# A fused attention, rational layer and expert layer on one core: weight conversion with PSUM banks and tiles of its own, weight words off GpSimd, two first steps moved, planner constants changed

## The chip, the core and the metric

The kernel runs on one core of a Trainium2 chip. The time is device microseconds of one execution; the kernel before is shown with the median of three runs and with one profiled execution, whose trace all rows below come from. In the rows, PE is TensorE's matmuls and PEld its weight loads, DVE is VectorE, ACT is ScalarE, POOL is GpSimd and SP is SyncE, which issues most DMAs.

## What is computed

Three layers follow each other. The first is a recurrence over 768 positions for 32 heads with a complex decay of bounded magnitude; the kernel computes it as chunked attention. The second is a rational function between two products (384 to 2048 to 384). The third routes each of the 3072 rows to one of eight experts and computes that expert's two products (384 to 1024 to 384).

```python
def _moe_ref(x, w_in, w_out, a, b):
    h = x @ w_in
    h2 = h * h
    h3 = h2 * h
    P = a[0] + a[1] * h + a[2] * h2 + a[3] * h3
    Q = 1.0 + np.abs(b[0]) * np.abs(h) + np.abs(b[1]) * h2
    g = P / (Q + 1e-06)
    return (g @ w_out).astype(np.float32)

def _moe2_ref(x, expert_emb, tau, w1, w2):
    xn = x / (np.linalg.norm(x, axis=-1, keepdims=True) + 1e-06)
    en = expert_emb / (np.linalg.norm(expert_emb, axis=-1, keepdims=True) + 1e-06)
    logits = xn @ en.T / tau
    expert_idx = np.argmax(logits, axis=1)
    ...
    for e in range(E):
        mask = expert_idx == e
        h = np.maximum(x[mask] @ w1[e], 0.0)
        out[mask] = gate_w[mask, None] * (h @ w2[e])
```

The weights of the rational layer come as 64 bit floats and are turned into 32 bit floats on the chip.

## The kernel before

The program is one straight line of instructions for each engine. Their order is written by a planner, `Plan`: a stage adds operations with an engine (or a choice of engines), an estimated duration, what they read and write, a due time, and sometimes a PSUM bank to take and to give back. `emit` then walks an estimated clock, takes among the operations that could start soonest the one with the earliest due time, and where there is a choice takes the engine with the lowest price (`price` times duration) or, if the operation is late, the one that ends first by estimate plus `bias`. An operation can only go where the planner put it: each engine works through its own list in order. There are two plans that matter here, one for `attention` and one for `mixture` (the rational layer and the expert slots); all of attention's instructions stand ahead of the mixture's in each engine's list.

**Attention** goes through 24 chunks of 128 rows. Its SBUF tiles come from three pools `a_p0` to `a_p2`, its eight PSUM banks from one pool `a_ps` that all of its steps share. Beside the chunks, `weight` (L680 on) converts the 32 weight tiles: a DMA into one of two `raw` tiles, an absolute value on ScalarE into one of two `wa` tiles, four VectorE steps through one bank, and for `w_out` a transpose and a small product, each with a bank of its own. The result lies in the `wf` tiles.

**The rational layer** runs over eight blocks of 384 columns with eight units each, 64 units in all. A unit (`unit`, L1020 on) is a first product `mm1` (18 matmuls, L1018) into one of the two `ph` banks pairs, six ScalarE and five VectorE steps (L1041 to L1053), and a second product `mm2` (18 matmuls, L1063) that is summed over the eight units in the `acc` banks. Unit 2 alone uses two `acc` banks for its first product. Numbers are split into a high and a low word: `split` (L1002) makes the high word `wh` by a cast (helper line L210) and the low word by a subtraction (L212) for each weight tile. Ten of the 32 tiles are split at the end of attention, 22 (11 high, 11 low) in this stage. `xsplit` does the same for a block of x (L229, L233). The planner's mark `free` stands for the release of attention's tiles and comes 9 us into the stage by its clock; it is an entry of the plan, not an instruction.

When a stage ends, its pools are released, and tiles of the next stage are laid over them; the first use of the new tile waits for the last users of what lay there. `mixture` takes its pools in the order `m_t`, `m_x`, `m_w`, `m_wh`, `m_g`, `m_r`, and its eight banks from one pool `m_ps`.

**The expert slots** follow: groups of 256 rows of one expert are gathered by GpSimd (L1358), transposed through `acc` banks (L1376), split (L982, L1381), multiplied with split weights (`slot_split`, L1414 for the low words) and scattered to the output (L1418). A small block for the last few rows of experts (L1548 to L1581) runs beside them.

```python
    def split(n):
        i, nm, lo = PARTS[n]
        on = [("A", 0.73), ("V", 0.47)] if not lo else [("V", 0.87), ("G", 1.76)]
```

## Time and profile before

| what | us |
|---|---|
| median of three runs | 945.04 |
| lowest and highest of them | 943.94, 947.12 |
| the profiled execution | 946.07 |
| its span, first to last instruction | 944.2 |

The rows below are read by stage. A busy time is the part of a stretch in which at least one instruction of the engine runs; the number in brackets is how many started there. PEclk is the granted clock of TensorE as a share of its higher level, 2.4 GHz; 0.50 is the lower level, 1.2 GHz, for the whole stretch. In a timeline, the brackets at the end of a row tell how long the engine stood idle before the instruction and whose work ended that.

### The profile page before, as it was taken

The numbers are of one execution on the slowest core, as the hardware profiler recorded it, in microseconds if no ns is written. First come the engines' busy times: TensorE is split into PE (matmuls) and PEld (weight loads), VectorE is DVE, ScalarE is ACT, GpSimd is POOL, SyncE is SP. The second block draws the span as 40 slices with busy tenths as digits, with TensorE's granted clock in tenths as the row PEclk, the third lists the DMA queues.
The fourth block names the chain that finished last, engine by engine and source line by source line (L and its number), as shares of the span: only waits on it lengthen the run. The fifth ranks groups of instructions, "written<-read, shape, count | busy, mean of one in ns | idle before, by whom it ended". The sixth has DMA issues, their size and how long they took to land. (4 is left out here: it accounts for less than half of the span.)

```text
span 944.2 us, 16850 instructions
## 1 busy us (share of the span) xinstructions
PE 877.2 (93%) x6119; PEld 834.0 (88%) x6119; DVE 738.1 (78%) x1419; ACT 704.3 (75%) x1134; POOL 237.1 (25%) x184
## 2 busy tenths in 40 slices
PE   2999999989879999999999999999998979999994
PEld 2788988878779999999999999999998878788994
DVE  7989998989799879787978888796987866556530
ACT  7989998989586988888988888888653543545530
POOL 2425434555254110001001010101322232225311
PEclk9999999989889999999999999999999998999997
DMA  9989988884200000010100000033202156551400
GB/s 174 200 174 175 184 187 175 151 188 100 85 1 1 1 26 1 1 26 1 26 1 26 1 27 1 16 77 94 35 9 60 51 163 204 171 168 37 168 26 27
DMA packets 172865, 76.41 MB, mean 81 GB/s; under 512 B 140840, under 2 KB 167352, under 8 KB 172772
## 3 DMA queue, kind: packets, MB, share of 16 engines
q1 hardware_dynamic: 168804, 65.58, 31.4%
q0 software_dynamic: 3968, 9.66, 3.6%
q8 instruction: 50, 0.82, 0.4%
q14 instruction: 43, 0.35, 0.2%
HBM read 92.19 MB, written 9.96 MB: 108 GB/s over the span
## 5 line engine op out<-in xcount | busy, mean ns | idle before, releaser
L1018 PE MATMUL ph<-xh,wi 128*128 128x384 f32 (+1 forms) x1284 | 306.2, 317 | 8.3 <-DVE wfi L490 4.2
L1018 PEld LDWEIGHTS ph<-xh,wi 128*128 128x128 f32 x1284 | 223.7, 190 | 10.3 <-DVE wfi L490 4.4
L1063 PE MATMUL acc<-wo,gh 128*128 128x392 f32 x768 | 202.0, 344 | 4.1 <-ACT gh L1052 4.1
L1018 PE MATMUL ph<-xl,wi 128*128 128x384 f32 (+1 forms) x642 | 203.1, 316 | 0.0
L1063 PEld LDWEIGHTS acc<-wo,gh 128*128 128x128 f32 x768 | 141.2, 190 | 4.4 <-ACT gh L1052 4.4
L1063 PE MATMUL acc<-wo,gl 128*128 128x392 f32 x384 | 131.7, 343 | 2.5 <-DVE gl L1053 2.5
L1018 PEld LDWEIGHTS ph<-xl,wi 128*128 128x128 f32 x642 | 122.0, 190 | 0.0
L1126 POOL DMA_INDIRECT idl<-tok,pos x24 | 24.6, 1026 | 281.4 <-DVE pos L1123 177.4
L1063 PEld LDWEIGHTS acc<-wo,gl 128*128 128x128 f32 x384 | 72.7, 189 | 3.3 <-DVE gl L1053 3.3
L1461 PE MATMUL acc<-wo,gh 128*128 128x384 f32 x256 | 70.0, 354 | 3.4 <-DVE wo L1414 3.4
L1053 DVE TENSOR_TENSOR gl<-u,gh 128x768 fp32r<-128x768 f32 x48 | 47.0, 979 | 27.1 <-PE acc L1063 26.2
L1041 ACT ACTIVATE sq<-ph,quad 128x768 f32<-128x768 f32 x43 | 38.8, 902 | 30.3 <-PE ph L1018 27.3
L1449 ACT ACTIVATE gh<-ph 128x512 fp32r<-128x512 f32 x36 | 21.6, 599 | 52.6 <-PE ph L1018 31.3
L1461 PEld LDWEIGHTS acc<-wo,gh 128*128 128x128 f32 x256 | 45.8, 194 | 9.1 <-issue 4.6
L499 ACT COPY qkT<-bank 96x512 f32<-96x512 f32 x96 | 50.7, 587 | 3.4 <-PE bank L621 3.0
L1418 POOL DMA_INDIRECT out_dram<-ah,ido x24 | 27.3, 1137 | 99.5 <-ACT ah L1466 55.2
L1358 POOL DMA_INDIRECT xT<-x2d,ids x24 | 27.2, 1134 | 98.9 <-DVE oh L1104 45.9
L630 PE MATMUL bank<-qkT 96*128 96x128 f32 x384 | 50.7, 279 | 1.3 <-ACT qkT L499 1.3
L1046 DVE SCALAR_TENSOR_TENSOR u<-u,qtmp,ph 128x768 f32<-128x768 f32 x47 | 47.2, 1005 | 5.4 <-ACT u L1044 5.3
L620 PE MATMUL bank<-cst,qf 128*96 128x128 f32 x192 | 48.2, 290 | 2.9 <-ACT qkT L499 2.9
L630 PEld LDWEIGHTS bank<-qkT 96*128 96x128 f32 x384 | 46.9, 193 | 2.8 <-ACT qkT L499 2.5
L1049 DVE SCALAR_TENSOR_TENSOR sq<-sq,quad,ah 128x768 f32<-128x768 f32 x43 | 46.6, 1084 | 0.6 <-ACT ah L1048 0.5
(298 smaller groups left out, 2160.6 us busy)
## 6 DMA issues: line engine op xcount, KB each, us to landing
xT<-in_moe_w_dram SPq DMA_DIRECT2D x24, 1536.0 KB
mw<-in_moe_w_dram SPq DMA_DIRECT2D x32, 384.0 KB
raw<-in_moe_w_out_dram SPq DMA_DIRECT2D x16, 384.0 KB
raw<-in_moe_w_in_dram SPq DMA_DIRECT2D x16, 384.0 KB
x2d<-rows SPq DMA_DIRECT2D x24, 192.5 KB
a_re<-in_a_re_dram SPq DMA_DIRECT2D x24, 192.0 KB
a_im<-in_a_im_dram SPq DMA_DIRECT2D x24, 192.0 KB
k<-in_k_dram SPq DMA_DIRECT2D x24, 192.0 KB
```

What stands on the lines that cost most here:

```text
L499: (A.copy if e == "A" else eng[e].tensor_copy)(o, i)
L620: T.transpose(pv[:, i, 0, :], Q[:, 2 * j + i, :], ident)
L630: T.matmul(pb(b)[:, i * P:(i + 1) * P], O[:, i, 1, :], O[:, i, 0, :], start=True, stop=True)
L1018: T.matmul(o, l, r, start=(n == 0), stop=(n == len(steps) - 1))
L1041: add(("A", 0.81 if many else 0.45), lambda e, c=c, h=h: A.activation(z[:, c], h(), AF.Abs, scale=coef.kb), w=kh + kz_)
L1046: add(("V", 0.93 if many else 0.53), lambda e, c=c, h=h: V.scalar_tensor_tensor(out=w[:, c], in0=w[:, c], scalar=coef.d, in1=h(), op0=ALU. ...
L1049: add(("V", 0.93), lambda e: V.scalar_tensor_tensor(out=z, in0=z, scalar=coef.e, in1=s, op0=ALU.add, op1=ALU.mult), r=ks, w=kz_)
L1053: add(("V", 0.87), lambda e: V.tensor_tensor(out=l, in0=w, in1=g.bitcast(F32), op=ALU.subtract), r=kw + kg, w=kl, lat=0.27)
L1063: T.matmul(o, x[:, j, sl], y("o", i)[:, c], start=(i == 0 and j == 0 and k == 0), stop=(i == NP - 1 and j == 1 and k == 2))
L1358: G.indirect_dma_start(out=xg[i][t], out_offset=None, in_=x2d[0:n, :], in_offset=bass.IndirectOffsetOnAxis(ap=ids[i][:, t:t + 1], axis=0), ...
L1418: G.indirect_dma_start(out=out[:, :], out_offset=bass.IndirectOffsetOnAxis(ap=dst, axis=0), in_=src, in_offset=None, bounds_check=NT - 1, ...
L1461: T.matmul(o, x[:, j, sl], w[:, c], start=(q == 0 and j == 0 and n == 0), stop=(q == NQ - 1 and j == 1 and n == 2))
```

## The change

- In attention, the PSUM pool is divided: six banks (`B`) for the chunks, two (`W`, a pool `a_psw`) for all banks that weight conversion takes. The tiles `raw` and `wa` come from a pool `a_w` that is allocated first.
- In `mixture`, `m_x` (the second x block) is allocated first and `m_t` second, so that `m_x` lies where `a_w` was. Two of the four `acc` banks come from a pool `m_psc` and lie where `a_psw` was; the two `ph` pairs and the other `acc` banks from `m_ps`.
- `split` has no choice of engine any more: high words on ScalarE, low words on VectorE.
- The memset of `seen` and the cast of `tok` were written ahead of the plan; they are now operations of it behind `free`. The split of x block 1 waits for `free` too.
- The planner's prices, biases and due times have new values.

```diff
-PRICE = {'A': 0.9451088, 'G': 0.6799360, 'V': 1.1, 'T': 0.0, 'S': 0.0}
+PRICE = {'A': 0.9451088, 'G': 0.5023880, 'V': 1.1, 'T': 0.0, 'S': 0.0}
-BIAS = {'A': -0.0773127, 'G': 0.1603192, 'V': 0.6045377, 'T': 0.0, 'S': 0.0}
+BIAS = {'A': -0.0215282, 'G': 0.2572650, 'V': 0.6045377, 'T': 0.0, 'S': 0.0}
-COST = {'A': 0.7094815, 'G': 0.3193946, 'V': 1.1, 'T': 0.0, 'S': 0.0}
-LEAN = {'A': 0.1119026, 'G': 0.1802717, 'V': 0.4995443, 'T': 0.0, 'S': 0.0}
-SPREAD = 0.0605191
+COST = {'A': 0.4040183, 'G': 0.5656184, 'V': 1.1, 'T': 0.0, 'S': 0.0}
+LEAN = {'A': -0.0850600, 'G': -0.1987378, 'V': 0.0905153, 'T': 0.0, 'S': 0.0}
+SPREAD = 0.1250329
-LEAN_FROM = 4.5359957
+LEAN_FROM = 3.1556660
...
-    STEP, SLACK, HALVED = 5.3246472, 0.0630705, (1,)
-    pools = [ctx.enter_context(tc.tile_pool(name=f"a_p{i}", bufs=1)) for i in range(3)]
-    ps = ctx.enter_context(tc.tile_pool(name="a_ps", bufs=1, space=PSUM))
+    NWB = 2
+    STEP, SLACK, HALVED = 5.3419923, 0.0630705, (1,)
+    late, *pools = (ctx.enter_context(tc.tile_pool(name=f"a_{n}", bufs=1)) for n in ("w", "p0", "p1", "p2"))
+    ps, psw = (ctx.enter_context(tc.tile_pool(name=n, bufs=1, space=PSUM)) for n in ("a_ps", "a_psw"))
...
-    raw = new("raw", [P, 384, 2], U32, c=2)
+    raw = [late.tile([P, 384, 2], U32, name=f"raw{i}") for i in range(2)]
-    wa = new("wa", [P, DM], c=2)
+    wa = [late.tile([P, DM], F32, name=f"wa{i}") for i in range(2)]
-    banks = [ps.tile([P, 512], F32, name=f"bank{i}") for i in range(8)]
...
+    banks = [(ps if i < 8 - NWB else psw).tile([P, 512], F32, name=f"bank{i}") for i in range(8)]
+    plan = Plan({"B": range(8 - NWB), "W": range(8 - NWB, 8)}, SimpleNamespace(price=PRICE, bias=BIAS, margin=MARGIN, start=START, chain=0.2, warm=0.0, port=True, lat=0.2))
...
-        ts(0.47, t, hi, 3, 0x3FFFFFFF, ALU.logical_shift_left, ALU.bitwise_and, kr, [bw], take=("B", bw))
+        ts(0.47, t, hi, 3, 0x3FFFFFFF, ALU.logical_shift_left, ALU.bitwise_and, kr, [bw], take=("W", bw))
-            add(("T", 0.33), trans, r=["cst", key], w=[bt], take=("B", bt))
+            add(("T", 0.33), trans, r=["cst", key], w=[bt], take=("W", bt))
-            add(("T", 0.59), dots, r=["wT", "en_T"], w=[be], take=("B", be))
+            add(("T", 0.59), dots, r=["wT", "en_T"], w=[be], take=("W", be))
...
-    UNIT, GROUP = 6.0000, 16.4000
+    UNIT, GROUP = 7.2713966, 12.6223970
-    DELAY = -0.4256865
-    RAMP = 1.5
+    DELAY = -1.0923189
+    RAMP = 1.5540458
-    AHEAD = 6.0
-    BEFORE = 8.0
-    FETCH = 0.0
+    AHEAD = 8.1409276
+    BEFORE = 10.2176109
+    FETCH = -0.1452395
-    tp, xs.pool = pool("m_t"), pool("m_x")
+    xs.pool, tp = pool("m_x"), pool("m_t")
-    ps = ctx.enter_context(tc.tile_pool(name="m_ps", bufs=1, space=PSUM))
+    ps, psc = (ctx.enter_context(tc.tile_pool(name=n, bufs=1, space=PSUM)) for n in ("m_ps", "m_psc"))
-    banks = [ps.tile([P, 512], F32, name=f"acc{i}") for i in range(4)]
+    banks = [(ps if i < 2 else psc).tile([P, 512], F32, name=f"acc{i}") for i in range(4)]
...
-        on = [("A", 0.73), ("V", 0.47)] if not lo else [("V", 0.87), ("G", 1.76)]
+        on = ("A", 0.75) if not lo else ("V", 0.9)
-            add([("A", 0.41), ("V", 0.27)], lambda e, kk=kk: xs.hi(eng[e], b, kk), r=["xT"], w=[("x", b % 2, 0, kk)])
+            add([("A", 0.41), ("V", 0.27)], lambda e, kk=kk: xs.hi(eng[e], b, kk), r=["xT"] + ["free"] * (b == 1), w=[("x", b % 2, 0, kk)])
-    V.memset(seen[0][:, 0, :], 0.0)
-    V.tensor_copy(tok, cc(C_TOK, NG))
+            add(("G", 1.04), lambda e, t=t: scatter(e, t), r=["pos", "tok"], w=[("idl", t)], lat=6.5, due=UNIT * NP * (b + 1) + (14.0 if last else 40.0))
+        vop(lambda: V.memset(seen[0][:, 0, :], 0.0), r=["free"], w=[("seen", 0)])
+        vop(lambda: V.tensor_copy(tok, cc(C_TOK, NG)), r=["free"], w=["tok"])
```

## Rows read from the trace of the kernel before

**Rows 1.** The page: its first line.

```profile
span 944.2 us, 16850 instructions
```

**Rows 2.** Busy time by stage: start and end, length, busy us (instructions), clock, DMA.

```profile
60.00:249.00 189.00, 182.28 (x1746) 162.35 (x1746) 170.56 (x314) 174.89 (x334) 91.75 (x64) 0.98 0.78 161
249.00:320.00 71.00, 58.55 (x291) 56.76 (x292) 63.29 (x66) 53.00 (x69) 25.90 (x11) 0.88 0.03 10
320.00:655.00 335.00, 335.00 (x1908) 335.00 (x1907) 278.03 (x502) 290.06 (x409) 21.15 (x21) 1.00 0.09 22
655.00:925.00 270.00, 255.38 (x1818) 240.25 (x1817) 174.08 (x409) 134.82 (x223) 76.86 (x61) 0.98 0.33 97
```

**Rows 3.** Busy time of three stretches inside the passage, columns as in rows 2.

```profile
253.00:258.00 5.00, 4.88 (x15) 4.88 (x16) 0.11 (x3) 1.34 (x3) 0.00 (x0) 0.50 0.19 51
...
272.00:282.00 10.00, 5.00 (x16) 4.27 (x15) 9.75 (x10) 6.55 (x9) 2.57 (x2) 0.66 0.00 0
...
306.00:320.00 14.00, 12.06 (x60) 11.74 (x59) 12.83 (x14) 13.86 (x18) 2.60 (x1) 0.88 0.01 2
```

**Rows 4.** TensorE's timeline, 249 to 320: start, us, work [idle before <-who ended it].

```profile
253.12 0.69 PE L1018 MATMUL ph<-xh,wi 128*128 128x384 f32 x1 [4.18 <-DVE wfi L490]
...
276.30 1.02 PE L1063 MATMUL acc<-wo,gh 128*128 128x392 f32 x2 [4.10 <-ACT gh L1052]
...
308.34 0.44 PE L1018 MATMUL ph<-xh,wi 128*128 128x384 f32 x1 [1.94 <-DVE gl3s L1046]
```

**Rows 5.** VectorE's timeline at the head of the passage.

```profile
257.96 0.07 DVE L1075 MEMSET seen<- 128x8 f32 x1 [4.89 <-DMA xT<-y]
...
264.23 0.56 DVE L210 CAST wo<-wfo 128x784 fp32r<-128x784 f32 x1
...
265.18 2.64 DVE L1049 SCALAR_TENSOR_TENSOR sq<-sq,quad,ah 128x768 f32<-128x768 f32 x1
```

**Rows 6.** GpSimd's timeline in the same place.

```profile
264.93 4.61 POOL L212 TENSOR_TENSOR wo<-wfo,wo 128x784 fp32r<-128x784 f32 x2 [1.97 <-DVE wo L210]
```

**Rows 7.** VectorE's groups, 249 to 320: count, busy us, mean ns, idle before.

```profile
L1049 DVE SCALAR_TENSOR_TENSOR sq<-sq,quad,ah 128x768 f32<-128x768 f32 x6 | 9.3, 1551 | 0.0
L1050 DVE SCALAR_TENSOR_TENSOR sq<-sq,ah 128x768 f32<-128x768 f32 x6 | 8.0, 1337 | 0.0
...
L210 DVE CAST wi<-wfi 128x768 fp32r<-128x768 f32 x5 | 6.0, 1221 | 0.0
L210 DVE CAST wo<-wfo 128x784 fp32r<-128x784 f32 x6 | 5.7, 966 | 0.0
L1051 DVE SCALAR_TENSOR_TENSOR u<-u,quad,sq 128x768 f32<-128x768 f32 x4 | 5.6, 1394 | 0.0
L1051 DVE SCALAR_TENSOR_TENSOR gl3s<-gl3s,quad,sq 128x768 f32<-128x768 f32 x2 | 3.5, 1738 | 0.0
...
L1049 DVE SCALAR_TENSOR_TENSOR gh3s<-gh3s,quad,gl2s 128x768 f32<-128x768 f32 x2 | 2.0, 1008 | 0.0
...
L1050 DVE SCALAR_TENSOR_TENSOR gh3s<-gh3s,gl2s 128x768 f32<-128x768 f32 x2 | 1.9, 951 | 0.0
```

**Rows 8.** ScalarE's timeline in the passage: its longest wait.

```profile
297.74 0.84 ACT L1052 CAST gh<-gl3s 128x768 fp32r<-128x768 f32 x1 [6.39 <-DVE gl3s L1051]
```

**Rows 9.** VectorE's groups in the slots, 655 to 925: low words of slot weights.

```profile
L1414 DVE TENSOR_TENSOR wi<-xT,wi 128x768 fp32r<-128x768 f32 x40 | 37.0, 950 | 1.8 <-ACT wi L982 1.1 <-issue 0.6
```

**Rows 10.** Groups of all engines, 340 to 600: ScalarE's cast of 768 elements.

```profile
L1052 ACT CAST gh<-u 128x768 fp32r<-128x768 f32 x31 | 25.7, 828 | 1.3 <-PE acc L1063 1.2
```

**Rows 11.** GpSimd's groups, whole span: one of three of slot low words.

```profile
L1414 POOL TENSOR_TENSOR wi<-xT,wi 128x768 fp32r<-128x768 f32 x4 | 9.3, 2326 | 24.6 <-ACT wi L982 24.6
```

**Rows 12.** TensorE's timeline in the slots: the longest idle place there.

```profile
779.01 0.90 PE L1548 MATMUL acc<-cst,rows 128*128 128x128 f32 x3 [6.37 <-DVE xl L1381]
```

**Rows 13.** VectorE's timeline ahead of that place.

```profile
774.93 3.56 DVE L1414 TENSOR_TENSOR wo<-xT,wo 128x768 fp32r<-128x768 f32 x4
778.41 1.01 DVE L1381 TENSOR_TENSOR xl<-acc,xh 128x384 fp32r<-128x384 f32 x2
```

More of the change, by code (lines that the diff above doesn't have):

```diff
@@ L463, in attention @@
     head = lambda t, h: t[:, h * D:h * D + 64]
-    banks = [ps.tile([P, 512], F32, name=f"bank{i}") for i in range(8)]
-    plan = Plan({"B": range(8)}, SimpleNamespace(price=PRICE, bias=BIAS, margin=MARGIN, start=START, chain=0.2, warm=0.0, port=True, lat=0.2))
+    banks = [(ps if i < 8 - NWB else psw).tile([P, 512], F32, name=f"bank{i}") for i in range(8)]
+    plan = Plan({"B": range(8 - NWB), "W": range(8 - NWB, 8)}, SimpleNamespace(price=PRICE, bias=BIAS, margin=MARGIN, start=START, chain=0.2, warm=0.0, port=True, lat=0.2))
     pb = lambda key: banks[plan.bank[key][1]]
@@ L945, in mixture @@
     NQ = NF2 // 2
-    UNIT, GROUP = 6.0000, 16.4000
-    LAG = 6.0
+    UNIT, GROUP = 7.2713966, 12.6223970
+    LAG = 6.0000000
     FIRST = 2
-    DELAY = -0.4256865
-    RAMP = 1.5
+    DELAY = -1.0923189
+    RAMP = 1.5540458
     LATER = 1.0
-    AHEAD = 6.0
-    BEFORE = 8.0
-    FETCH = 0.0
+    AHEAD = 8.1409276
+    BEFORE = 10.2176109
+    FETCH = -0.1452395
     pool = lambda n: ctx.enter_context(tc.tile_pool(name=n, bufs=1))
-    tp, xs.pool = pool("m_t"), pool("m_x")
+    xs.pool, tp = pool("m_x"), pool("m_t")
     parts.pools = pool("m_w"), pool("m_wh")
@@ L1131, in route @@
         for t in range(TPB):
-            add(("G", 1.04), lambda e, t=t: scatter(e, t), r=["pos"], w=[("idl", t)], lat=6.5, due=UNIT * NP * (b + 1) + (14.0 if last else 40.0))
+            add(("G", 1.04), lambda e, t=t: scatter(e, t), r=["pos", "tok"], w=[("idl", t)], lat=6.5, due=UNIT * NP * (b + 1) + (14.0 if last else 40.0))
         for t in range(TPB):
```

## The prediction, made before the changed kernel was run

> **What bounds the kernel now.** I read the span first [rows 1], then the busy time of each engine by stage [rows 2], then the idle places of TensorE, one by one, in its timeline, and behind each the engine that ended it. The stages are: attention with the conversion of the rational layer's weights (0 to 249 us), the passage into the rational layer (249 to 320), the rational layer in steady flow (320 to 655), the expert slots (655 to 925), the last rows going out.
>
> The reader is to see in [rows 2] that TensorE is the bound, but not everywhere. From 320 to 655 it is busy 335.0 of 335 us at clock 1.00 and starts 1908 matmuls, 5.70 per us: nothing around it can be worth anything there. In the passage it starts 291 in 71 us; at 5.70 per us they need 51.1 us, so **19.9 us are lost in the passage**. The same loss comes out of its parts: idle 71 - 58.55 = 12.45 us, and clock: 4.88 us of work at 0.50 is 2.4 us lost, a mean of 0.66 over 10 us is 3.4, of 0.88 over 14 us is 1.7 [rows 3]; together 19.9. Each idle place is followed by matmuls at the lower of the two clock levels.
>
> Who ends the idle places? [rows 4]: the first unit's matmuls begin 4.18 us late, on VectorE's last weight word (wfi L490), although their own inputs are long there: all eight PSUM banks belong to one pool, and the wait is for the last user of that pool. The next, 4.10 us, waits for gh L1052 of the first unit, and 1.94 us at 308 for a VectorE step (L1046). So behind the passage stands VectorE. It is late for two reasons. It stands still for 4.9 us in front of a 65 ns memset of `seen`, waiting for the last transfer of y into xT [rows 5]. And it runs slowly beside GpSimd: from 264.93 on GpSimd makes low words (L212), and in that time one step on VectorE takes 2.64 us [rows 5, 6], against 1.01 elsewhere in the same stage [rows 7]. A cast of a high word takes 0.56 us where it is left alone, and 1.22 or 0.97 in the mean [rows 5, 7]. ScalarE in turn waits 6.39 us at one place for VectorE [rows 8].
>
> **The change, part by part.**
>
> *The pools.* Weight conversion gets two banks and its SBUF tiles raw and wa a pool of their own; in the next stage only two accumulators and the second x block come to lie on them. The first matmuls then wait for the other six banks, whose last user is the copy of the last y, just behind the end of attention's matmuls at 249. That removes most of 4.18 us and the 2.4 us of low clock behind it; it costs no instruction. The other side is attention: six banks instead of eight for its own chain. Conversion has only two raw buffers, so at most two conversions are under way in either kernel, and two banks are enough for them; the w_out words also take a bank each for a transpose and a small product. From 60 to 249 TensorE idles 189 - 182.28 = 6.7 us [rows 2]. Bounds: all of it gone (-6.7) or doubled (+6.7); I take 0, since nothing in the trace says which.
>
> *The moved first steps.* The memset and the cast of `tok` go from the head of VectorE's queue to behind the planner's `free` mark (9 us into the stage). VectorE loses its 4.9 us standstill; the two steps themselves (0.25 us) are needed only by the first route, some 50 us later, and no DMA goes with them. The three splits of x block 1 also move behind that mark; they are needed by unit 8, about 50 us into the stage, which covers them. Cost 0; without that cover it would be three ScalarE copies and three VectorE steps, some 3 us.
>
> *Weight words without GpSimd.* Before, all 11 high words that are left for this stage are VectorE casts (L210, 5 and 6) [rows 7], and the 11 low words are GpSimd's 11 instructions [rows 2]. Now the high words go to ScalarE and the low words to VectorE. For VectorE:
> - taken away: the stretch beside GpSimd. Six L1049 at 1.551 instead of 1.008 is 3.3 us, six L1050 at 1.337 instead of 0.951 is 2.3, four L1051 at 1.394 and two at 1.738 instead of the same 1.008 are 1.5 and 1.5, eleven casts at 1.221 and 0.966 instead of 0.56 are 3.3 and 2.4 [rows 5, 7]: 14.3 us. With the standstill 19.2 us, which is about what TensorE loses.
> - removed 11 casts at 0.56, 6.2 us; added 11 low words at 0.95, the mean of the same shape and form in the slots [rows 9], 10.5 us: net 4.3 us to pay.
> - left: 19.2 - 4.3 = **14.9 us**.
>
> For ScalarE: 11 casts at 0.83 [rows 10], 9.1 us more. It is busy 53.0 of 71 us [rows 2], so 18.0 us are free. If the stage becomes shorter by G, 18.0 - 9.1 - G are left: nothing at G = 8.9. Beyond that its work runs over into the steady flow, where it has 335 - 290.06 = 45 us free.
>
> So the gain of the passage lies between 8.9 us (ScalarE may not run over at all) and 19.9 (everything lost comes back). VectorE's sum says 14.9, at which ScalarE runs over by 14.9 + 9.1 - 18.0 = 6.0 us. TensorE can take part of this, because it works on three or four units ahead of the elementwise chain. I take a third of it, 2 us, as new idle time: **13 us**.
>
> By a rule of the Trainium skill, "VectorE: DVE Perf Modes", section "The perf-mode tier table", an fp32 copy from SBUF runs at twice the rate of a two-input step on VectorE; the change gives up just this fast form for the high words. The rows agree (0.56 against 0.95), and ScalarE needs 0.83 for the same words, 11 x 0.27 = 3.0 us dearer. By the rule alone, with the dearer engine as the bound, the gain would be 3 us less; which would bring it near the first rival below; the sum stands without it.
>
> *The constants.* They set the planner's order and, where an instruction may go to two engines, the engine. In the steady flow they can change nothing: TensorE is at 335 of 335. In the slots TensorE idles 270 - 255.38 = 14.6 us [rows 2]. The dearer price of GpSimd sends the slots' low words to VectorE: GpSimd has nine of them now (four stand in [rows 11]), so 9 x 0.95 = 8.6 us, hidden by VectorE's 270 - 174.08 = 96 free us unless they stand ahead of something urgent. The due times of slots and their splits move too. Bounds: -14.6 (all idle time gone) to +18.8 (two more stalls like the worst one, below); I take 0, the order of now being my only evidence.
>
> **Sum.** The profiled execution took 946.07 us, its span 944.2 [rows 1]. 944.2 - 13 = 931.2, with 1.9 outside the span 933.1. The median of the runs lies 1.03 below the profiled one: **932 us**. From 320 on TensorE has no idle time, so what the passage gives is handed to the end in full.
>
> **The rivals.**
> - *ScalarE takes VectorE's place.* The high words fall due when the first eight units need ScalarE most; none of its work can be put off. Gain 8.9: 936. For it: 62 us of work in a stage that would be 58 long. Against: its idle time comes in pieces of 4 to 6 us in front of VectorE's results, which is what goes.
> - *The slots get better too*: half of their 14.6 us goes: 932 - 7.3 = 925.
> - *It does not do what it says*: the six banks, or the tiles of the next stage, still wait for something that ends at 253 to 258, and the chain of the first unit finds ScalarE occupied: the idle places move but stay. 945. Against it: VectorE's stretch is GpSimd's alone, and GpSimd is out.
> - *Slower: the slots stall on VectorE's low words.* At 779 TensorE stood for 6.37 us with all four accumulator banks held by transposed rows; the two xl steps that free them (L1381) stood in VectorE's queue behind four low words [rows 12, 13]. With GpSimd's nine low words on VectorE as well, and splits due earlier, this can happen again in other slots. A stall costs 6.4 us and 2.4 to 3.4 of low clock behind it, as in [rows 3]: 9.4. Two more make +18.8 - 13 = +5.8: 951. It decides from 13 / 9.4 = 1.4 on: one more stall still leaves the kernel faster, two do not. Against: the xl steps also fall due 2.2 us earlier, and VectorE has 96 us free.
>
> **How the numbers follow.** Forecast (gain 13, with attention and slots within some 5 us) 0.52; ScalarE 0.15; better slots 0.12; no effect 0.07; slower 0.14. Range: the first four lie from 925 to 945, with the bound of 6.7 us for attention on the low side of the forecast and of the third case the range goes from 917 to 945; outside remain the slower case and a little of the third, under 2 in 10. A measurement of this kernel can tell about 0.3% (2.8 us) from no change. Faster by more: 0.52 + 0.15 + 0.12 = 0.79; within: 0.07; slower: 0.14.
>
> **What would show it.** In the changed trace, between 248 and 320: the first L1018 within 1 us of attention's last matmul, at clock 1.00; no L212 on GpSimd; no VectorE step of 768 elements over 1.1 us; the memset of `seen` without a wait before it; TensorE idle under 5 us instead of 12.45. ScalarE should have almost no idle time from 252 to 310; if TensorE waits there for ScalarE's gh (L1052), the first rival is at work. The slots' low words all on VectorE; a stall of L1548 or L1461 behind L1381 or L1414 longer than the present ones is the last rival. Wrong altogether would be a passage that still loses 15 us, or an attention stage whose end moves by more than 7 us from 249.

## The result and the profile after

The changed kernel takes 923.37 us (median of four, 920.63 to 924.49) where the kernel before, on the same chip, takes 946.08 (943.94 to 947.29): a ratio of **0.976, interval 0.974 to 0.978**. Forecast were 932.0 us and a range from 917 to 945. The profiled execution took 923.47 us.

The page's first line, then the busy time by stage with the columns of [rows 2]; the last stretch ends earlier because the kernel does.

```profile
span 921.7 us, 16828 instructions
...
60.00:249.00 189.00, 181.15 (x1710) 158.79 (x1711) 169.28 (x307) 173.88 (x331) 89.26 (x63) 0.98 0.76 159
249.00:320.00 71.00, 67.63 (x400) 65.51 (x399) 65.72 (x87) 65.84 (x89) 0.00 (x0) 1.00 0.05 14
320.00:655.00 335.00, 335.00 (x1913) 334.93 (x1912) 279.63 (x522) 293.13 (x419) 29.35 (x25) 1.00 0.16 21
655.00:905.00 250.00, 244.05 (x1767) 228.86 (x1766) 161.29 (x378) 132.01 (x217) 54.31 (x48) 1.00 0.34 106
```

In the passage TensorE starts 400 matmuls instead of 291, at full clock, and GpSimd does nothing there. (Some 40 of the 400 are left over from attention, which ends a little later.) In the slots it idles 250 - 244.05 = 6 us where it idled 14.6, and the clock is 1.00 instead of 0.98 [rows 2].

What is left of the idle places in the passage, from TensorE's timeline, 249 to 320, as in [rows 4]:

```profile
253.25 0.45 PE L1019 MATMUL ph<-xh,wi 128*128 128x384 f32 x1 [0.78 <-ACT y L504]
268.11 0.44 PE L1019 MATMUL ph<-xh,wi 128*128 128x384 f32 x1 [1.57 <-DVE u L1047]
275.08 0.62 PE L1064 MATMUL acc<-wo,gh 128*128 128x392 f32 x2 [0.27 <-ACT gh L1053]
276.34 0.45 PE L1064 MATMUL acc<-wo,gl 128*128 128x392 f32 x1 [0.64 <-DVE gl L1054]
```

The 4.18 and 4.10 us are gone; the first matmul now waits 0.78 us for the copy of the last y (L504), as the divided banks were to make it. (Lines are one higher than before: L1049 of [rows 7] is L1050 here.)

VectorE's and ScalarE's groups in the same stretch, columns as in [rows 7]:

```profile
L1050 DVE SCALAR_TENSOR_TENSOR sq<-sq,quad,ah 128x768 f32<-128x768 f32 x7 | 7.1, 1014 | 0.5 <-ACT ah L1049 0.4
L1051 DVE SCALAR_TENSOR_TENSOR sq<-sq,ah 128x768 f32<-128x768 f32 x7 | 6.7, 951 | 0.0
L212 DVE TENSOR_TENSOR wo<-wfo,wo 128x784 fp32r<-128x784 f32 x6 | 5.8, 969 | 2.4 <-ACT wo L210 2.3
L212 DVE TENSOR_TENSOR wi<-wfi,wi 128x768 fp32r<-128x768 f32 x5 | 4.7, 952 | 0.2 <-ACT wi L210 0.2
L210 ACT CAST wo<-wfo 128x784 fp32r<-128x784 f32 x6 | 5.1, 848 | 0.0
L210 ACT CAST wi<-wfi 128x768 fp32r<-128x768 f32 x5 | 4.1, 834 | 0.0
```

VectorE's steps are back from 1.551 and 1.337 us to 1.014 and 0.951, each low word costs 0.95 to 0.97, each high word 0.83 to 0.85 on ScalarE: the sizes the prediction took from [rows 7, 9, 10]. ScalarE is full from 260 to 300 (columns of rows 2):

```profile
260.00:280.00 20.00, 17.40 (x94) 15.97 (x93) 17.73 (x21) 20.00 (x28) 0.00 (x0) 1.00 0.01 3
280.00:300.00 20.00, 20.00 (x115) 20.00 (x115) 19.82 (x26) 20.00 (x27) 0.00 (x0) 1.00 0.00 1
```

In the slots all 96 low words are VectorE's (88 of them in the two rows; GpSimd has no L1413), and the longest stall is 2.33 us instead of 6.37 [rows 12]:

```profile
L1413 DVE TENSOR_TENSOR wi<-xT,wi 128x768 fp32r<-128x768 f32 x44 | 40.9, 949 | 1.1 <-ACT wi L983 1.0
L1413 DVE TENSOR_TENSOR wo<-xT,wo 128x768 fp32r<-128x768 f32 x44 | 40.5, 949 | 6.0 <-ACT wo L983 6.0
...
692.22 0.44 PE L1460 MATMUL acc<-wo,gl2e 128*128 128x384 f32 x1 [2.33 <-DVE gl2e L1449]
```

**Where the time went.** Both kernels issue 6119 matmuls, so the start of the n-th can be compared. Matmul 2000 ends up in the last part of attention (242 us before), 2368 at the end of the passage (320), 4276 at the head of the slots (656), 5000 and 5120 before and behind the stall of [rows 12], 6100 near the end (927). A negative number is time gained by the changed kernel over the kernel before, in one trace each:

| matmul | start before | changed, lag in us |
|---|---|---|
| 2000 | 242.1 | +2.9 |
| 2368 | 320.2 | -11.7 |
| 4276 | 655.6 | -12.1 |
| 5000 | 770.0 | -15.9 |
| 5120 | 794.8 | -24.4 |
| 6100 | 926.9 | -23.5 |

From 2000 to 2368 the **passage gains 14.6 us**, the steady flow passes it on unchanged, and the **slots gain another 11.4**. The 2.9 us lost in attention are discussed below.

The table also tells where in the slots the gain comes. Of the 11.4 us, 3.8 come ahead of matmul 5000 and 8.4 between 5000 and 5120, at the place of the 6.37 us stall [rows 12] and its low clock; behind it, 0.9 us are lost again. The low words of the kernel before lie elsewhere (min/median/max ns, first and last start):

```profile
L1414 DVE TENSOR_TENSOR wi<-xT,wi x40: 931/950/961, 678.0 to 895.3; 128x768 fp32r<-128x768 f32 x40
L1414 POOL TENSOR_TENSOR wi<-xT,wi x4: 2052/2281/2689, 665.9 to 872.0; 128x768 fp32r<-128x768 f32 x4
L1414 POOL TENSOR_TENSOR wo<-xT,wo x3: 1848/1853/2057, 807.9 to 882.9; 128x768 fp32r<-128x768 f32 x3
L1414 POOL TENSOR_TENSOR wi_1b<-xT,wi_0b x2: 1854/1862/1871, 854.8 to 887.6; 128x768 fp32r<-128x768 f32 x2
```

Seven of GpSimd's nine start after 807 us, where nothing is gained, and none between 700 and 807; of VectorE's 40 words in the first row not one took over 0.96 us. One place fits GpSimd's company: beside its word of 665.89 a small VectorE step took 1.82 us, TensorE idled 1.58 us at 671, and the changed kernel gains 2 to 3 us around there. But most of the gain in the slots is one stall less, and that stall stood behind VectorE's own words [rows 13]; under the new constants VectorE's queue has another order.

### The profile page after: what moved, and what is told of

Read it like the earlier page. It is cut to its first block, busy times and chain, and to the rows that moved or that the text cites. A ratio compares the mean times of both kernels' runs of the same rounds, so it can differ in the third digit from the quotient of the medians.

```text
span 921.7 us, 16828 instructions
## 1 busy us (share of the span) xinstructions
PE 870.1 (94%) x6119; PEld 824.4 (89%) x6119; DVE 729.3 (79%) x1421; ACT 715.4 (78%) x1153; POOL 192.4 (21%) x163
## 5 line engine op out<-in xcount | busy, mean ns | idle before, releaser
L1019 PE MATMUL ph<-xh,wi 128*128 128x384 f32 (+1 forms) x1284 | 303.0, 315 | 2.9 <-DVE u L1047 1.6
L1019 PEld LDWEIGHTS ph<-xh,wi 128*128 128x128 f32 x1284 | 221.4, 188 | 6.3 <-DVE u L1047 2.3
L1064 PEld LDWEIGHTS acc<-wo,gh 128*128 128x128 f32 x768 | 139.7, 188 | 0.6 <-ACT gh L1053 0.6
L1125 POOL DMA_INDIRECT idl<-tok,pos x24 | 27.3, 1138 | 362.2 <-DVE lm L1144 141.7
L1460 PE MATMUL acc<-wo,gh 128*128 128x384 f32 x256 | 66.8, 342 | 0.0
L1047 DVE SCALAR_TENSOR_TENSOR u<-u,qtmp,ph 128x768 f32<-128x768 f32 x47 | 47.4, 1009 | 11.8 <-ACT u L1045 11.6
L1045 ACT ACTIVATE u<-ph,quad 128x768 f32<-128x768 f32 x47 | 46.3, 985 | 0.7 <-DVE gl L1054 0.7
L1460 PEld LDWEIGHTS acc<-wo,gh 128*128 128x128 f32 x256 | 44.5, 188 | 2.3 <-issue 2.3
## 6 DMA issues: line engine op xcount, KB each, us to landing
x2d<-rows SPq DMA_DIRECT2D x24, 192.5 KB
```

The costliest lines, as they stand in the source:

```text
L1019: T.matmul(o, l, r, start=(n == 0), stop=(n == len(steps) - 1))
L1045: add(("A", 0.9 if many else 0.5), lambda e, c=c, h=h: A.activation(w[:, c], h(), AF.Square, scale=coef.k, bias=coef.m), w=kh + kw)
L1047: add(("V", 0.93 if many else 0.53), lambda e, c=c, h=h: V.scalar_tensor_tensor(out=w[:, c], in0=w[:, c], scalar=coef.d, in1=h(), op0=ALU. ...
L1064: T.matmul(o, x[:, j, sl], y("o", i)[:, c], start=(i == 0 and j == 0 and k == 0), stop=(i == NP - 1 and j == 1 and k == 2))
L1125: G.indirect_dma_start(out=idl[t][:, :], out_offset=bass.IndirectOffsetOnAxis(ap=pos[:, t:t + 1], axis=0), in_=tok[:, b * TPB + t:b * TPB ...
L1460: T.matmul(o, x[:, j, sl], w[:, c], start=(q == 0 and j == 0 and n == 0), stop=(q == NQ - 1 and j == 1 and n == 2))
```

## The experiments

Theory at the time: GpSimd's weight words stretch VectorE's steps; take them off GpSimd, and the passage and the slots gain; what decides the engine is the planner's price. Rivals: ScalarE becomes the bound; the pools or the moved steps are what counts; the due times carry the slots.

Every run is set against the kernel before on the same chip. The two gains are differences of the lags above, from one trace each: passage is 2368 less 2000, slots is 6100 less 4276.

| kernel | us | ratio, interval | passage | slots |
|---|---|---|---|---|
| changed | 923.37 | 0.976 (0.974 to 0.978) | -14.6 | -11.4 |
| no_split | 920.82 | 0.976 (0.973 to 0.980) | -14.5 | -11.4 |
| no_banks | 926.23 | 0.982 (0.978 to 0.985) | -13.6 | -11.0 |
| no_moved | 923.52 | 0.979 (0.975 to 0.983) | -13.0 | -11.5 |
| no_consts_mix | 938.52 | 0.996 (0.993 to 0.999) | -14.1 | +5.3 |
| idle_words | 928.11 | 0.980 (0.976 to 0.984) | -9.9 | -11.1 |
| words_gpsimd | 932.5 | 0.982 (0.979 to 0.984) | -6.8 | -11.0 |
| old_due | 927.91 | 0.977 (0.975 to 0.980) | -14.0 | -6.3 |
| old_price | 967.93 | 1.019 (1.016 to 1.022) | -14.2 | +33.3 |
| high_on_vector | 938.88 | 0.988 (0.985 to 0.992) | -12.1 | +0.7 |
| only_consts_mix | 925.34 | 0.975 (0.971 to 0.978) | -12.2 | -9.7 |
| no_consts_att | 936.38 | 0.985 (0.981 to 0.988) | -15.3 | -2.3 |
| late_load | 932.28 | 0.979 (0.976 to 0.983) | -15.4 | -3.6 |

All but only_consts_mix are edits of the changed kernel; diffs are against it, except where said. In the kernels that keep the changed kernel's banks, words and first steps, the passage column lies between -14.0 and -15.4, so a difference of 1 us there can hardly be told from none.

### no_split: the choice of engines back

```diff
-        on = ("A", 0.75) if not lo else ("V", 0.9)
+        on = [("A", 0.73), ("V", 0.47)] if not lo else [("V", 0.87), ("G", 1.76)]
```

> The changed kernel (923.4 us) with the choice of engines in split as before: high words on ScalarE or VectorE, low words on VectorE or GpSimd, all else as changed. My theory (VectorE is slowed beside GpSimd's low words, and that was most of what the passage lost): if the planner gives the low words back to GpSimd, VectorE steps of 2.0 to 2.6 us come back between 255 and 315 and the time rises by 8 to 12 us, to 931 to 935. Rival (the pools and the moved steps gave the passage's gain): the stretched steps come back, but the time rises by less than 3 us, to under 926.

Nothing came back: the planner, with its new prices, put the words on the same engines, and GpSimd stays empty in the passage. The edit did not undo what it was meant to undo. The fixed engines are redundant beside the new prices; words_gpsimd below is the real undoing.

### no_banks: one PSUM pool, raw and wa among attention's tiles

```diff
-    late, *pools = (ctx.enter_context(tc.tile_pool(name=f"a_{n}", bufs=1)) for n in ("w", "p0", "p1", "p2"))
-    ps, psw = (ctx.enter_context(tc.tile_pool(name=n, bufs=1, space=PSUM)) for n in ("a_ps", "a_psw"))
+    pools = [ctx.enter_context(tc.tile_pool(name=f"a_p{i}", bufs=1)) for i in range(3)]
+    ps = ctx.enter_context(tc.tile_pool(name="a_ps", bufs=1, space=PSUM))
```

> The changed kernel with one PSUM pool of eight banks and raw and wa in the first pool, as before; split, moved steps and constants as changed. My theory: the first L1018-type matmul waits again for VectorE's last weight word, 3 to 4 us behind attention's last matmul, with 2.4 us of low clock behind it: plus 6 us, 929. Rival (in the passage ScalarE is the bound now, and TensorE's later start is absorbed): under plus 2 us, 925 or less.

The wait for VectorE's last weight word is back, 2.60 us instead of 4.18, with 3.4 us of low clock behind it. TensorE's timeline of this kernel:

```profile
255.53 0.44 PE L1018 MATMUL ph<-xh,wi 128*128 128x384 f32 x1 [2.60 <-DVE wfi L490]
```

The ratio is 0.006 above the changed kernel's, with intervals that meet at 0.978, and the passage 1.0 us worse: between theory and rival. The banks do what they say, for 1 to 5 us; most of that wait is made up later in the passage.

### no_moved: memset and cast at the head again, x block 1 without `free`

```diff
+    V.memset(seen[0][:, 0, :], 0.0)
+    V.tensor_copy(tok, cc(C_TOK, NG))
```

> The changed kernel with the memset of seen and the cast of tok back at the head of VectorE's list and the x block 1 split without its wait. My theory (each of VectorE's lost us counts): VectorE stands still for some 5 us in front of the memset until y's last transfer has landed, and the time rises by 3 to 5 us, to 927. Rival (ScalarE is the bound of the passage after the change, with 20.00 of 20 us busy, and VectorE has room): under plus 2 us, 925 or less.

VectorE stands still again and starts its first weight word at 261.8 instead of 256.55, but TensorE idles only 3.08 us at 265 instead of 1.57:

```profile
265.54 0.44 PE L1019 MATMUL ph<-xh,wi 128*128 128x384 f32 x1 [3.08 <-DVE u L1047]
```

The passage is 1.6 us worse, the ratio 0.003, inside the intervals: the rival, that VectorE had room, was nearer. The 4.9 us standstill of [rows 5] cost little.

### no_consts_mix: all constants of the mixture's plan old

```diff
-COST = {'A': 0.4040183, 'G': 0.5656184, 'V': 1.1, 'T': 0.0, 'S': 0.0}
+COST = {'A': 0.7094815, 'G': 0.3193946, 'V': 1.1, 'T': 0.0, 'S': 0.0}
...
-    UNIT, GROUP = 7.2713966, 12.6223970
+    UNIT, GROUP = 6.0000, 16.4000
```

> The changed kernel with the planner's constants of the mixture (engine prices, biases, slack, due times) as before; attention's constants, pools, split and moved steps as changed. My theory (the 11.3 us that the slots gained are the new order and engines there): the passage keeps its gain, the slots lose theirs, with idle places like the 3.4 and 6.4 us ones of the kernel before: 933 to 936. Rival (the slots gained because they are reached in another state, not through the constants): 923 to 926.

The passage keeps its gain, the slots lose all of theirs and 5.3 us more: the constants, which the prediction put at 0, are worth 16.7 us of slots here. GpSimd has 14 low words in the slots, and steps on VectorE are stretched beside them. Two of the six `seen` steps (L1109, 0.17 us elsewhere) took 1.80 and 1.73 us beside GpSimd's words at 680.61, and TensorE waited for them (groups, 600 to 925, mean ns behind the comma; then TensorE's timeline):

```profile
L1413 DVE TENSOR_TENSOR wi<-xT,wi 128x768 fp32r<-128x768 f32 x37 | 35.7, 995 | 3.3 <-ACT wi L983 3.3
L1413 POOL TENSOR_TENSOR wi<-xT,wi 128x768 fp32r<-128x768 f32 x7 | 15.4, 2213 | 4.5 <-ACT wi L983 4.4
L1413 POOL TENSOR_TENSOR wo<-xT,wo 128x768 fp32r<-128x768 f32 x4 | 11.6, 2894 | 14.2 <-issue 7.4 <-DVE xT L994 4.1 <-ACT wo L983 2.6
...
L1413 DVE TENSOR_TENSOR wo_1b<-xT,wo_0b 128x768 fp32r<-128x768 f32 x2 | 3.5, 1742 | 2.4 <-ACT wo_0b L983 2.4
L1109 DVE TENSOR_TENSOR seen<-seen,oh 128x8 f32<-128x8 f32 x6 | 4.2, 695 | 0.1
...
682.49 0.62 PE L1114 MATMUL acc<-seen,cst 128*128 128x24 f32 x2 [1.57 <-DVE seen L1109]
```

With a wait of 2.10 us just ahead, another of 1.14 behind and the low clock after them, this kernel loses some 8 us on the changed one around that place, by the start of the n-th matmul. The other half of the 16.7 us lies between 5000 and 5120, where it gains 0.8 us on the kernel before and the changed kernel 8.4.

### idle_words: work on GpSimd whose results nobody reads

Twelve subtractions of 720 elements on GpSimd in the passage, everything else as in the changed kernel.

```diff
+                idle.append(parts.room(31, F32R, "idle")[:, :720])
+            G.tensor_tensor(out=idle[0], in0=cst[:, 0:720], in1=cst[:, 4:724], op=ALU.subtract)
...
+        for n in range(12):
+            add(("G", 0.1), beside, w=["idle"], port=False)
```

> The changed kernel (923.4 us; 920.8 with the same passage and the choice of engines) with twelve subtractions of 720 elements on GpSimd at the head of the rational layer, whose results nobody reads; the order on the other engines is kept. It adds GpSimd's company alone, without moving any of VectorE's or ScalarE's work. My theory (GpSimd's two-input words slow VectorE's steps with two SBUF inputs): VectorE steps L1050, L1051, L1052, L1054 and L212 of 2.0 to 2.6 us between 253 and 285, some 14 us of stretch, of which VectorE had about 5 us free: plus 7 to 12 us, 930 to 935. Rival (the stretch comes from something else, or VectorE has room): under plus 3 us.

GpSimd is busy 22.1 us with them, VectorE's steps beside them lengthen, one stall of 4.56 us appears on TensorE, and the passage is 4.7 us worse. No data passes from these words to anything, and the other compute engines run the same instructions in the same order, so this is GpSimd's presence alone. In sum VectorE's steps took 6.9 us longer, not the 14 of the expectation, and the 4.7 us lie between the theory's 7 to 12 and the rival's 3. The kernel's groups and TensorE's timeline:

```profile
L1606 POOL TENSOR_TENSOR idle<-cst 128x720 fp32r<-128x720 f32 x12 | 22.1, 1838 | 5.8 <-PE bank L649 4.9
L1050 DVE SCALAR_TENSOR_TENSOR sq<-sq,quad,ah 128x768 f32<-128x768 f32 x7 | 8.8, 1259 | 0.5 <-ACT ah L1049 0.4
L212 DVE TENSOR_TENSOR wi<-wfi,wi 128x768 fp32r<-128x768 f32 x5 | 7.2, 1462 | 0.3 <-ACT wi L210 0.3
L1047 DVE SCALAR_TENSOR_TENSOR u<-u,qtmp,ph 128x768 f32<-128x768 f32 x8 | 8.1, 1007 | 0.2 <-ACT u L1045 0.2
...
269.57 0.69 PE L1019 MATMUL ph<-xh,wi 128*128 128x384 f32 x1 [4.56 <-DVE u L1047]
```

### words_gpsimd: the old placement, forced

```diff
-        on = ("A", 0.75) if not lo else ("V", 0.9)
+        on = ("V", 0.47) if not lo else ("G", 1.76)
```

> The changed kernel with the 11 high words forced to VectorE and the 11 low words to GpSimd, which is where the kernel before had them; pools, moved steps and constants as changed. In the run with only the choice given back the planner did not use it, so this is the real undoing. My theory: VectorE steps of 2.0 to 2.6 us come back and the passage loses 8 to 14 us against the changed kernel: 931 to 937. Rival (the pools carry the passage): under plus 4 us, 927.

The passage loses 7.8 us of its 14.6, just below the lower end of what was expected. The 4.10 us stall behind gh of [rows 4] is back at 4.08. VectorE's timeline, then a row each of GpSimd's and TensorE's, in this kernel:

```profile
260.06 2.22 DVE L210 CAST wo<-wfo 128x784 fp32r<-128x784 f32 x1
...
266.20 2.64 DVE L1050 SCALAR_TENSOR_TENSOR sq<-sq,quad,ah 128x768 f32<-128x768 f32 x1
268.76 1.00 DVE L1047 SCALAR_TENSOR_TENSOR u<-u,qtmp,ph 128x768 f32<-128x768 f32 x1
269.69 1.68 DVE L1051 SCALAR_TENSOR_TENSOR sq<-sq,ah 128x768 f32<-128x768 f32 x1
...
265.95 4.60 POOL L212 TENSOR_TENSOR wo<-wfo,wo 128x784 fp32r<-128x784 f32 x2 [1.96 <-DVE wo L210]
...
277.32 1.02 PE L1064 MATMUL acc<-wo,gh 128*128 128x392 f32 x2 [4.08 <-ACT gh L1053]
```

The two GpSimd words lie at 265.95 (2.07 us) and 267.98 (2.57). L1050 starts inside the first and ends 0.8 us after its end; L1051 starts inside the second and ends 0.8 us after its end: both wait for the word and then run. L1047 between them, which reads one operand from a PSUM bank (ph), takes its usual 1.00. The Trainium skill, "SBUF — State Buffer", section "Who interferes with whom", states this rule: a VectorE instruction with two SBUF inputs contends with a GpSimd instruction that reads SBUF, under an exclusive lock, and one with at most one SBUF input, outside the modes that use two ports, does not; it names casts among those that can enter such a mode. The trace agrees in all four rows of VectorE: the cast at 260.06, which takes 0.56 us alone [rows 5], started inside a GpSimd word that began at 259.81, and took 2.22.

### old_due and old_price: the two kinds of constants apart

```diff
-    UNIT, GROUP = 7.2713966, 12.6223970
+    UNIT, GROUP = 6.0000, 16.4000
...
-    AHEAD = 8.1409276
-    BEFORE = 10.2176109
+    AHEAD = 6.0
+    BEFORE = 8.0
```

> The changed kernel with the due-time constants of the mixture (unit, group, delay, ramp, ahead, before, fetch) as before, engine prices and biases as changed. All mixture constants as before gave 938.5. If the due times carry the slots' gain: 933 to 940. If the prices do (low words of the slots off GpSimd): 921 to 927.

With the old due times and the new prices the slots lose 5.1 us in the trace; the ratio is only 0.001 above the changed kernel's. The due times are worth 1 to 5 us.

```diff
-COST = {'A': 0.4040183, 'G': 0.5656184, 'V': 1.1, 'T': 0.0, 'S': 0.0}
-LEAN = {'A': -0.0850600, 'G': -0.1987378, 'V': 0.0905153, 'T': 0.0, 'S': 0.0}
+COST = {'A': 0.7094815, 'G': 0.3193946, 'V': 1.1, 'T': 0.0, 'S': 0.0}
+LEAN = {'A': 0.1119026, 'G': 0.1802717, 'V': 0.4995443, 'T': 0.0, 'S': 0.0}
```

> The changed kernel with the engine prices, biases and slack of the mixture as before, due-time constants as changed. If the prices carry the slots' gain: 933 to 940, with GpSimd making low words of slots again. If the due times do: 921 to 927; in that case GpSimd should make hardly any low words, since with the later due times no operation counts as late and the lowest price decides.

With the old prices and the new due times the kernel is slower than before, which neither side of the expectation had. GpSimd makes 72 of the 96 low words of the slots, at 2 us each, and one wait of TensorE, 8.56 us, is longer than any in the other kernels. Its two longest waits end on steps of VectorE, and 5.6 us in all on GpSimd's words; how the 33.3 us divide was not measured (groups, 600 to 960, and TensorE's timeline):

```profile
L1413 POOL TENSOR_TENSOR wo<-xT,wo 128x768 fp32r<-128x768 f32 x34 | 67.8, 2006 | 56.5 <-issue 16.4 <-DVE ids L1317 13.9 <-DVE wo L983 9.4
L1413 POOL TENSOR_TENSOR wi<-xT,wi 128x768 fp32r<-128x768 f32 x35 | 67.3, 1952 | 3.8 <-ACT wi L983 3.7
...
665.25 0.58 PE L1019 MATMUL ph<-xh,wi 128*128 128x256 f32 x1 [5.05 <-DVE gl3s L1047]
...
704.66 0.69 PE L1460 MATMUL acc<-wo,gl 128*128 128x384 f32 x1 [8.56 <-DVE gl L1449]
```

The planner's code explains why the words go there, which is argued and was not measured apart; the same prices also choose between ScalarE and VectorE for casts. A low word costs 1.1 x 0.87 = 0.957 on VectorE, and on GpSimd 0.319 x 1.76 = 0.56 by the old price, 0.566 x 1.76 = 0.996 by the new one. With the old due times most words were late, and a late word goes where it ends first. With the new ones they are in time, the lowest price decides, and the old price says GpSimd. By this argument the two must fit each other, and the price decides the engine.

### high_on_vector: high words back on VectorE

```diff
-        on = ("A", 0.75) if not lo else ("V", 0.9)
+        on = ("V", 0.47) if not lo else ("V", 0.9)
```

> The changed kernel with the high words of the passage's weights back on VectorE (0.56 us each by its casts) and the low words left on VectorE: VectorE gets 22 casts, some 12 us, that ScalarE made (0.84 us each, some 18 us). Theory, ScalarE is the passage's tightest engine after the change and VectorE, at 65.7 of 71 us busy there, is close behind it: VectorE is now the bound, 65.7 + 12 is 6 to 7 us more than the stretch holds, so the passage ends 4 to 9 us later and the ratio to the kernel before is 0.981 to 0.986. Rival, VectorE's work in the passage has slack in its order and ScalarE is what TensorE waits for: the passage ends up to 3 us earlier, ratio 0.973 to 0.976.

The expectation counted 22 casts; there are 11 (VectorE's groups show 6 and 5), so 6 us and not 12 move to VectorE, and the 4 to 9 us were too many. The passage is 2.5 us worse, in the direction of the theory, with VectorE at 69.12 of 71 us:

```profile
249.00:320.00 71.00, 66.93 (x384) 64.60 (x383) 69.12 (x99) 59.88 (x78) 0.00 (x0) 0.98 0.04 12
```

So the rival, ScalarE, is not what sets the passage; VectorE is. The ratio of 0.988 lies above the 0.981 to 0.986 expected for another reason: the rest of the lost time begins with a stall at the seam to the slots, 659 us, which the next but one section meets again with the words in their new places.

### only_consts_mix: the kernel before with the mixture's new constants

Against the kernel before:

```diff
-COST = {'A': 0.7094815, 'G': 0.3193946, 'V': 1.1, 'T': 0.0, 'S': 0.0}
+COST = {'A': 0.4040183, 'G': 0.5656184, 'V': 1.1, 'T': 0.0, 'S': 0.0}
...
-    UNIT, GROUP = 6.0000, 16.4000
+    UNIT, GROUP = 7.2713966, 12.6223970
```

> The kernel before with the new prices and due times of the rational layer and the mixture, and nothing else of the change: one pool of banks, old place of the weight staging, old order of the first steps. Theory, these constants alone take the low words off GpSimd, in the passage (where the choice between the engines goes by the price) and in the slots, and carry most of the gain: 10 to 15 us in the passage's end, 8 to 12 us more in the slots, a ratio of 0.977 to 0.984. Rival, the pools and the moved steps are needed for the low words to leave GpSimd at a gain: the passage gains under 7 us and the ratio is 0.985 to 0.990.

Numbers alone give the whole gain: 0.975, with one pool of banks, the old places and the old first steps. GpSimd is empty in the passage, as the theory has it:

```profile
249.00:320.00 71.00, 65.75 (x363) 64.52 (x360) 62.86 (x79) 65.30 (x87) 0.00 (x0) 0.98 0.04 11
```

The parts do not add up: the new placement without the pools gives 12.2 us of the passage, the pools and moves without the new placement 6.8 (words_gpsimd), both together 14.6. TensorE still starts this passage 4.19 us late, and the chain behind makes it up.

### no_consts_att and late_load: attention's constants, and a stall at the seam

```diff
-PRICE = {'A': 0.9451088, 'G': 0.5023880, 'V': 1.1, 'T': 0.0, 'S': 0.0}
-BIAS = {'A': -0.0215282, 'G': 0.2572650, 'V': 0.6045377, 'T': 0.0, 'S': 0.0}
+PRICE = {'A': 0.9451088, 'G': 0.6799360, 'V': 1.1, 'T': 0.0, 'S': 0.0}
+BIAS = {'A': -0.0773127, 'G': 0.1603192, 'V': 0.6045377, 'T': 0.0, 'S': 0.0}
```

> The changed kernel with the attention's four old constants. Theory, they move nothing that bounds the attention: the first matmul of the rational layer comes within 3 us of the changed kernel's and the ratio is 0.974 to 0.978. Rival, they cost the 2.9 us that the changed kernel's trace was behind at the end of the attention: the ratio is 0.971 to 0.974, or they gain what another row hides and it is above 0.980.

The theory missed. Of the rival's two branches the ratio fits the second, above 0.980, but most of it comes from a place that neither named. Matmul 2000 comes 7.4 us later than before (changed kernel: 2.9), so the new constants give attention some 4.5 us in the two traces. And at the seam between the rational layer and the slots, TensorE stands 4.75 us for a gathered tile of tokens, with 6.8 us of low clock behind it; in the changed kernel the same matmul came without a wait:

```profile
665.95 0.87 PE L1375 MATMUL acc<-cst,xT 128*128 128x128 f32 x3 [4.75 <-DMA xT<-x2d,ids]
```

The instructions around that place stand in the same order on TensorE, SyncE and GpSimd in both kernels. What differs is SyncE's time: the changed kernel issues the three writes of `x2d` in 5.39 us, this one in 1.32, so that the 1.5 MB weight load behind them starts ahead of the last gather (646.2 there, 649.94 here) and not behind it. SyncE's timeline, first the changed kernel, then this one:

```profile
642.38 5.39 SPq L1150 DMA_DIRECT2D x2d<-rows  x3
648.01 11.94 SPq L1341 DMA_DIRECT2D xT<-in_moe_w_dram  x2
```

```profile
646.12 1.32 SPq L1150 DMA_DIRECT2D x2d<-rows  x3
647.68 16.01 SPq L1341 DMA_DIRECT2D xT<-in_moe_w_dram  x2
```

high_on_vector shows the same picture, with 1.32 us for the writes and a stall of 5.31 (there the profile puts the end of the wait down to a small VectorE step, `tab` L994, that ended just then). late_load puts eight small transfers ahead of that weight load in the kernel with attention's old constants:

```diff
+            if n and not s:
+                for j in range(8):
+                    SY.dma_start(idle[:, j:j + 1], w1v[0][:, 0, j:j + 1])
```

> The changed kernel with the attention's old constants (the kernel of the row before), and eight transfers of one word to each partition, whose data nothing reads, put on SyncE's queue just ahead of the second 1.5 MB weight load of the first slot, so that this load starts some 3 us later, behind the gathers of the tokens instead of ahead of them. Theory, with the old attention constants the load started at 647.7 us, 2.3 us ahead of the last gather, and the gathered tokens came late: TensorE stood 4.75 us at 661 and had 6.8 us of low clock behind it. With the load behind the gather this stall is under 1.5 us, no low clock follows it, and the ratio to the kernel before falls from 0.985 to 0.975 to 0.979. Rival, the gathered tokens are late for another reason (the old constants' own order): the stall stays over 4 us and the ratio stays at 0.983 to 0.988.

```profile
646.71 15.97 SPq L1345 DMA_DIRECT2D idle<-in_moe_w_dram  x8
...
663.49 0.87 PE L1380 MATMUL acc<-cst,xT 128*128 128x128 f32 x3 [3.07 <-DMA xT<-x2d,ids]
```

The row of the eight issues is 16 us long, not 3. Each took only 0.33 to 0.48 us to issue, but SyncE stood for 12.5 us in front of the last three, by the profile for the three writes of `x2d` to land (7.1 us at the longest). So the load started at 662.9, far behind the gather. The stall went from 4.75 to 3.07 us, the 6.8 us of low clock behind it stayed, and the ratio went from 0.985 to 0.979, with intervals that overlap: between theory and rival. The load ahead of the gather is at most a part of the cause. With that load not yet issued, the last of the writes still took some 16 us to land (issued at 646.35, the wait for it over at 662.36), and the gather was late. **What makes the writes and the gather slow in these kernels stays open**, as does why the three writes take 5.4 us to issue in one kernel and 1.3 in the other.

## Why the prediction was right, and where it was off

- **The number: inside the range, by a case that had little of the chance.** The forecast of 932, with 0.52, was a gain of 13 us with attention and slots within some 5 us. The slots gained 11.4, so what came is the rival "the slots get better too", with 0.12 and 925. That 923.4 lies so near 925 is luck in part: against that rival the passage gave 1.6 us more, the slots 4.1 more, and attention took back 2.9.
- **The passage: right.** Forecast 13 us, measured 14.6. VectorE's sum said 14.9. The 2 us taken off for ScalarE's overrun did not come: ScalarE is full from 260 to 300, but behind the first 0.78 us only 0.27 us of TensorE's idle time there ends on it. The bound of 8.9 us, and with it the rival "ScalarE takes VectorE's place", fell: its work ran over into the steady flow for nothing. That TensorE was already units ahead by then is the likely reason; it was not tested.
- **The mechanism behind that sum: right, its terms too large.** Of VectorE's sum, the stretch beside GpSimd less the 4.3 us of dearer words is 14.3 - 4.3 = 10.0 us; putting the words back costs 7.8 (words_gpsimd), idle work on GpSimd 4.7 (idle_words). The other term, the standstill of 4.9 us, was worth at most 1.6 (no_moved). The bank wait, which the sum leaves out, was worth 1.0 (no_banks). One at a time they come to 7.8 + 1.6 + 1.0 = 10.4 of the 14.6 us. So it is luck in part that the sum came within 0.3 us. The rest may lie in their overlap, where one part makes up for another that is undone; no run shows that apart.
- **Two readings that were off, without a part in the forecast.** The second way to the 19.9 us counts the low clock of 272 to 282 us over all 10 us, of which TensorE was idle for 5; on its 5.0 busy us the clock can have cost 2.5 and not 3.4, and the parts come to some 19. And "from 320 on TensorE has no idle time" holds to 655 only; the slots idle 14.6 us [rows 2]. The passage's gain did reach the end, with -11.7 at matmul 2368 and -12.1 at 4276.
- **High words on ScalarE: right.** The cast on VectorE is cheaper (0.55 us against 0.84), yet the passage with it is 2.5 us worse (high_on_vector): the engine with the cheaper cast was the one that bound.
- **Attention at 0: held within its bounds.** Matmul 2000 was 2.9 us late in the trace of the changed kernel; in the eight other kernels with the same attention instructions it lay between -0.7 and +5.7, so this is a scatter of single executions around some 2 us of loss. With the old constants and six banks it is 7.4 and 6.7 (no_consts_att, late_load), with the old constants and eight banks 0.4 (only_consts_mix): two banks fewer do cost attention, and the new constants seem to give most of it back.
- **Constants and slots at 0: the step that failed.** This term was mis-sized: it measured -11.4 us. The prediction took the order of the kernel before as its only evidence, though it knew that the constants set that order and had itself found the slots' worst stall, 6.37 us [rows 12], behind VectorE's own queue [rows 13]. It priced stalls that the new order adds, up to two; for one that goes it had only a rival, half of the idle time or 7.3 us, which names no stall. The stretch of this one, with the low clock behind it, is 8.4 of the 11.4 us. GpSimd's nine low words, on which it dwelt, carried little of it: most of the gain does not lie where they lie. The constants are shown to be the cause: without them the slots lose 5.3 us (no_consts_mix), with them alone they gain 9.7, of which 7.0 in the same stretch (only_consts_mix). Which of them removes the stall stays open. The slower rival's condition, words that pile up behind a wrong price, exists: old_price loses 33.3 us in the slots, with 72 words on GpSimd.
- **The signs named at its end** came out as said: first matmul 0.78 us after the last of attention, clock 1.00, no L212 on GpSimd, no VectorE step of 768 elements over 1.1 us, the memset without a wait, ScalarE busy 56.84 of the 58 us from 252 to 310, idle under 5 us (71 - 67.63 = 3.4).

## What to carry to other kernels

When one engine's instructions hold up another's, the cost is that of the neighbour's steps and not of its own: look for the steps with two SBUF operands that run twice as long in one stretch as elsewhere, and find who is busy there. In a planned kernel, read the prices as code: compute price times duration for each choice by hand, and ask for which operations the price decides and for which the lateness; here the numbers of the plan alone were worth the whole gain. Undo the parts of a large change one at a time before crediting any: here the numbers alone gave all of it, and the structural parts, each right in itself, 1 to 5 us. And look where along a stage the time is won, by the start of the n-th matmul, before giving it to a cause: here the words that left GpSimd are worth more than half of the passage, and most of the slots' gain is one stall less.

## What the runs showed of the hardware

- Beside GpSimd subtractions, VectorE's steps with two SBUF operands and its casts of fp32 from SBUF were held for whole instructions (0.95 to 1.01 us became up to 2.64, casts of 0.56 up to 2.22, a step of 128x8 went from 0.17 to 1.80); a step with a PSUM operand kept 1.00 us. In idle_words, 22.1 us of GpSimd work that nothing waits for lengthened VectorE's steps by 6.9 us in sum and the passage by 4.7.
- The same three 192.5 KB writes took 5.39 us to issue in one kernel and 1.32 in another with the same order of instructions around them (the second and third 2.4 us each, or 0.37). In late_load, where they took 1.32, the last of them landed some 16 us after its issue, and SyncE stood for 12.5 us in front of issues that waited for them.
